# Two batches side by side: attention in phases of its own, and one conversion of a weight chunk per two batches

## The chip, the cores and the metric

The kernel runs on one core of a Trainium2 chip. The metric is the device time of one execution in microseconds (us). The core has a matrix engine (TensorE, PE in the profile), two elementwise engines (VectorE, DVE; ScalarE, ACT), GpSimd (POOL), and SyncE (SP), which here only issues transfers (DMA).

## The reference

Four batches of 448 tokens go through sigmoid attention with 12 heads of 64, a token-shift block with gate, and a mixer over tokens and channels.

```python
scores = scale * np.matmul(q, k.transpose(0, 1, 3, 2)) - np.log(S)
attn = 1.0 / (1.0 + np.exp(-scores))
x = heads side by side of np.matmul(attn, v)              # (4, 448, 768)
xk = mu_k * x + (1.0 - mu_k) * x_prev                     # x_prev: x one token earlier
xr = mu_r * x + (1.0 - mu_r) * x_prev
k = np.maximum(xk @ w_k, 0.0)                             # (448, 1024)
x = 1.0 / (1.0 + np.exp(-(xr @ w_r))) * (k * k @ w_v)     # (448, 768)
h = np.maximum(x.transpose(0, 2, 1) @ w_tok1, 0.0) @ w_tok2
u = x + h.transpose(0, 2, 1)
out = u + np.maximum(u @ w_ch1, 0.0) @ w_ch2              # 768 -> 1536 -> 768
```

`w_k` and `w_r`, `w_v`, `w_tok1`, `w_tok2`, `w_ch1`, `w_ch2` come as 64-bit numbers and are turned into 32-bit ones on the chip.

## The kernel before, in words

Activations lie with channels on the 128 partitions and tokens along the columns; 448 columns are one batch. A product of two 32-bit matrices is made of three matmuls: each operand is split into a high part (rounded for the matmul's number type) and a low part (the rest), and high x high, high x low and low x high are summed in PSUM (lines 339, 341 and 342, `products`). Activations as operands are the tiles `Ah`/`Al` and `Mh`/`Ml`, weights `whi`/`wlo`.

Weights come in 52 chunks of 128 output columns (38 of them 128 x 768, 14 of 128 x 512). A chunk passes five steps: load of the 64-bit words (`raw`), two ACT operations that take them apart (`narrow_1`, lines 189 and 190), two DVE operations that join them (`narrow_2`, 193 and 196), ACT's copy to the high part (251), DVE's subtraction to the low part (256). Before, the first use of a chunk passes all five and stores the joined 32-bit chunk in DRAM (`kept`); later uses load it from there and pass the last two. `weights()` hands out the next chunk and lets the steps of the chunks behind it advance.

Stages ahead of the channels run per batch (`first_part`): r (w_r, 6 chunks), k (w_k, 8 chunks; relu, square, split), w_v (12 chunks of 512 rows, two per row of output, with transposes of the finished rows in between, line 392; in the last three batches two of six rows are transposed by DVE and small DMAs instead, `y_turn`), first token product (tok1), second token product (tok2). Channel mixing (`second_part`, ch1 and ch2 in two halves) runs for two batches side by side, in pieces of 512 and 384 columns; the first batch's rows wait in DRAM (`away`).

Attention: a unit is one pair of heads of one batch, 24 in all. `unit_qk` makes scores for 128 keys of both heads into a `psc` buffer (2 buffers) and ACT makes the sigmoid (line 154); `unit_av` multiplies by the values (163). Batch 0's attention runs first, by itself; the units of the later batches are put between the products by a planner (`spread`, `run`) that counts the time of the matmuls issued. Each engine runs its instructions in the order written; SP issues all transfers in order.

Of the kernel before, what the change touches and what calls it, by code (L numbers as in the profile page):

```python
# [47 lines left out]
BLK = 32
# [3 lines left out]
def kernel(  # L52
# [16 lines left out]

# [9 lines left out]
    const, big = pool("const", 1), pool("big", 1)  # L79
    wraw, wpool, wsplit = pool("wraw", 4), pool("wpool", 4), pool("wsplit", 3)  # L80
    dram = pool("dram", 1, space=bass.MemoryType.DRAM)
    tmps, tmp2 = pool("tmps", 4), pool("tmp2", 2)
    a3, a7 = pool("a3", 3), pool("a7", 7)
# [3 lines left out]
    def ENG(kind, b):  # L87
        return DVE if (kind, b) in ONDVE else ACT

    def split(hi, lo, src, engine):  # L90
        if engine is ACT:
            ACT.copy(hi, src)  # L92
        else:
            DVE.tensor_copy(hi, src)  # L94
        DVE.tensor_tensor(out=lo, in0=src, in1=hi.bitcast(F32), op=ALU.subtract)  # L95
# [4 lines left out]
    kns, qns, vns = {}, {}, {}  # L100

    def load_kq(g):
        if g < B * NPAIR:
            kns[g] = a3.tile([P, 4 * P], F32, tag="kn", name="kn")
            SP.dma_start(out=kns[g], in_=k[g])
            qns[g] = a3.tile([P, S], F32, tag="qn", name="qn")
            SP.dma_start(out=qns[g], in_=q[g])

    def load_v(g):
        if g < B * NPAIR:  # L110
            vns[g] = a3.tile([P, 2, 4, D], F32, tag="vn", name="vn")
# [15 lines left out]
    load_kq(1)  # L127

# [4 lines left out]
    for name, src in (("k", mu_k), ("r", mu_r)):  # L133
# [4 lines left out]
        mus[name] = (m, om)  # L138


    xe = big.tile([P, NT, 1 + S], F32, tag="xe", name="xe")
    POOL.memset(xe[:, :, 0:1], 0.0)

    att = {}

    def unit_qk(b, pr, chunks):
        g = b * NPAIR + pr
        for c in chunks:
            ps = ps_sc.tile([P, 2, 512], F32, tag="sc", name="psc")
            for h in range(2):  # L150
                me = slice(h * D, h * D + D)
                PE.matmul(ps[:, h, :S], kns[g][me, c * P : (c + 1) * P], qns[g][me], start=True, stop=True)  # L152
            a = a7.tile([P, 2, S], F32, tag="a", name="a")
            ACT.activation(a, ps[:, :, :S], AF.Sigmoid, bias=-math.log(S), scale=1.0 / math.sqrt(D))  # L154
            att[(g, c)] = a

    def unit_av(b, pr):
        g = b * NPAIR + pr
        ps = ps_av.tile([P, 512], F32, tag="av", name="pav")
        for c in range(4):  # L160
            a = att.pop((g, c))
            for h in range(2):
                PE.matmul(ps[h * D : h * D + D, :S], vns[g][:, h, c], a[:, h], start=(c == 0), stop=(c == 3))  # L163
        ACT.copy(xe[:, pr, 1:], ps[:, :S])

    def burst(b, pr):
        g = b * NPAIR + pr
        unit_qk(b, pr, (0, 1))
        load_kq(g + 2)
        load_v(g + 1)  # L170
        if pr:
            unit_av(b, pr - 1)
# [521 lines left out]
```

## Time and profile before

| | |
|---|---|
| median of 3 runs | 956.77 us (956.35 to 959.75) |
| the profiled execution | 958.75 us, its span 957.0 us |
| busy in the span | PE 918.9, weight loads 731.8 (they overlap PE), DVE 481.3, ACT 400.2 us |
| moved by DMA | 133.22 MB |

A matmul's busy time includes its way through the array and overlaps the next one's, so the time that one costs in a sequence is read from the distance of two starts. PEclk is the granted clock of TensorE as a share of 2.4 GHz.

### The profile page before, as it was taken

How to read it: one execution, taken by the hardware profiler on the slowest of the kernel's cores; microseconds unless marked ns; L12 is line 12 of the kernel's file. 1: busy time of each engine (PE TensorE's matmuls, PEld its weight loads, DVE VectorE, ACT ScalarE, POOL GpSimd, SP SyncE). 2: the span in 40 equal slices, each digit the busy share in tenths (PEclk: the TensorE clock that was granted, in tenths of full speed). 3: DMA queues.
4: the chain of work that ended last, by engine and by line, in shares of the span. 5: the costliest groups of instructions: out<-in, count | busy, mean ns of one | idle time of the engine just before them, and what ended most of it. 6: DMA issues, size and time to landing. Idle time of an engine off the chain costs nothing.

```text
span 957.0 us, 11625 instructions
## 1 busy us (share of the span) xinstructions
PE 918.9 (96%) x4484; PEld 731.8 (76%) x4484; DVE 481.3 (50%) x785; ACT 400.2 (42%) x622; POOL 1.3 (0%) x10
## 2 busy tenths in 40 slices
PE   9999998899999899999999999999899899999998
PEld 3367666687796687797988676677799788998987
DVE  3955675783234844444589224435835462232232
ACT  6767666424635654343521444433243342111210
POOL 0000000000000000000000000000000000000000
PEclk9999999999999999999999999999999999999999
DMA  8846556433336643655415532232423422142223
GB/s 290 277 167 230 186 183 208 151 107 114 99 100 214 228 164 131 213 168 197 158 62 179 184 98 87 77 86 67 149 89 87 134 96 68 61 144 69 66 75 106
DMA packets 59767, 133.22 MB, mean 139 GB/s; under 512 B 12352, under 2 KB 26176, under 8 KB 59712
## 3 DMA queue, kind: packets, MB, share of 16 engines
q1 hardware_dynamic: 59712, 132.48, 42.0%
q8 instruction: 35, 0.57, 0.3%
q14 instruction: 20, 0.16, 0.1%
HBM read 101.46 MB, written 29.62 MB: 137 GB/s over the span
## 4 chain that ended last, share of the span: by engine, by line
PE 80%; DVE 13%; ACT 4%; issue 3%; DMA 0%; SPq 0%; DVEq 0%; POOL 0%; ACTq 0%; POOLq 0%
PE psmm L342 21%; PE psmm L339 21%; PE psmm L341 20%; PE pav L163 8%; PE psc L152 8%; DVE wlo L256 3%; DVE mix L329 2%; DVE Al L95 2%; ACT Ah L92 1%; ACT a L154 1%; DVE Ah L94 1%; DVE wd L193 1%; DVE mix L328 1%; DVE r L495 1%; PE psmm L392 1%
## 5 line engine op out<-in xcount | busy, mean ns | idle before, releaser
L342 PE MATMUL psmm<-Ah,wlo 128*128 128x448 f32 (+2 forms) x688 | 250.9, 365 | 15.2 <-DVE wlo L256 15.2
L339 PE MATMUL psmm<-Ah,whi 128*128 128x448 f32 (+2 forms) x688 | 251.9, 366 | 1.9 <-DVE Ah L95 1.0
L341 PE MATMUL psmm<-Al,whi 128*128 128x448 f32 (+2 forms) x672 | 244.2, 363 | 0.2 <-DVE Al L95 0.2
L342 PE MATMUL psmm<-Mh,wlo 128*128 128x448 f32 (+2 forms) x480 | 176.7, 368 | 10.6 <-DVE wlo L256 10.5
L251 ACT CAST whi<-wd 128x768 fp32r<-128x768 f32 (+1 forms) x160 | 120.3, 756 | 138.0 <-PE psmm L341 102.8
L339 PE MATMUL psmm<-Mh,whi 128*128 128x448 f32 (+2 forms) x480 | 177.0, 369 | 0.5 <-DVE r L541 0.5
L341 PE MATMUL psmm<-Ml,whi 128*128 128x448 f32 (+2 forms) x480 | 175.3, 365 | 0.0
L256 DVE TENSOR_TENSOR wlo<-wd,whi 128x768 fp32r<-128x768 f32 (+1 forms) x160 | 136.8, 858 | 49.2 <-ACT whi L251 48.8
L342 PEld LDWEIGHTS psmm<-Ah,wlo 128*128 128x128 f32 x688 | 129.6, 188 | 30.6 <-DVE wlo L256 19.5
L339 PEld LDWEIGHTS psmm<-Ah,whi 128*128 128x128 f32 x688 | 129.6, 188 | 24.6 <-issue 10.5
L341 PEld LDWEIGHTS psmm<-Al,whi 128*128 128x128 f32 x672 | 126.7, 188 | 11.7 <-DVE Al L95 0.7
L342 PEld LDWEIGHTS psmm<-Mh,wlo 128*128 128x128 f32 x480 | 90.5, 188 | 24.5 <-DVE wlo L256 15.7
L154 ACT ACTIVATE a<-psc 128x896 f32<-128x896 f32 x96 | 82.9, 915 | 56.9 <-PE psc L152 56.9
L339 PEld LDWEIGHTS psmm<-Mh,whi 128*128 128x128 f32 x480 | 90.5, 188 | 13.7 <-issue 4.6
L341 PEld LDWEIGHTS psmm<-Ml,whi 128*128 128x128 f32 x480 | 90.6, 189 | 8.5
L152 PE MATMUL psc<-qn,kn 64*128 64x448 f32 x384 | 85.7, 565 | 2.9 <-ACT a L154 2.9
L527 DVE SCALAR_TENSOR_TENSOR Ml<-psmm,Mh 128x512 fp32r<-128x512 f32 (+1 forms) x48 | 29.9, 624 | 110.7 <-ACT Mh L526 110.7
L163 PE MATMUL pav<-a,vn 128*64 128x448 f32 x384 | 77.5, 545 | 0.0
L526 ACT ACTIVATE Mh<-psmm 128x512 fp32r<-128x512 f32 (+1 forms) x48 | 26.1, 544 | 108.2 <-PE psmm L342 108.2
L152 PEld LDWEIGHTS psc<-qn,kn 64*128 64x128 f32 x384 | 32.3, 185 | 48.6 <-issue 31.6
L163 PEld LDWEIGHTS pav<-a,vn 128*64 128x64 f32 x384 | 25.4, 136 | 48.0 <-issue 45.1
L193 DVE SCALAR_TENSOR_TENSOR wd<-wd,raw 128x768 uint32<-128x768 uint32 (+2 forms) x54 | 47.1, 872 | 3.5 <-ACT raw L190 3.4
(62 smaller groups left out, 599.6 us busy)
## 6 DMA issues: line engine op xcount, KB each, us to landing
wd<-w SPq DMA_DIRECT2D x66, 384.0 KB, 3.1
raw<-in_moe_w_ch_dram SPq DMA_DIRECT2D x24, 768.0 KB, 5.1
w<-wd SPq DMA_DIRECT2D x38, 384.0 KB, 3.1
wd<-w SPq DMA_DIRECT2D x42, 256.0 KB, 2.8
kn<-in_k_dram SPq DMA_DIRECT2D x24, 256.0 KB, 4.0
vn<-in_v_dram SPq DMA_DIRECT2D x24, 256.0 KB, 5.1
raw<-in_moe_w_k_dram SPq DMA_DIRECT2D x8, 768.0 KB, 5.9
raw<-in_moe_w_v_dram SPq DMA_DIRECT2D x12, 512.0 KB, 4.0
```

Source lines behind the costliest of these rows:

```text
L95: DVE.tensor_tensor(out=lo, in0=src, in1=hi.bitcast(F32), op=ALU.subtract)
L152: PE.matmul(ps[:, h, :S], kns[g][me, c * P : (c + 1) * P], qns[g][me], start=True, stop=True)
L154: ACT.activation(a, ps[:, :, :S], AF.Sigmoid, bias=-math.log(S), scale=1.0 / math.sqrt(D))
L163: PE.matmul(ps[h * D : h * D + D, :S], vns[g][:, h, c], a[:, h], start=(c == 0), stop=(c == 3))
L193: DVE.scalar_tensor_tensor(out=dst, in0=dst, scalar=3, in1=raw[..., 0], op0=ALU.logical_shift_left, op1=ALU.bitwise_or)
L251: ACT.copy(halves[i][0][:rows, :kt], loads[i])
L256: DVE.tensor_tensor(out=lo, in0=loads.pop(i), in1=f32(hi), op=ALU.subtract)
L339: PE.matmul(ps[:, :n], wh, xh, start=(i == 0), stop=False)
L341: PE.matmul(ps[:, :n], wh, xl, start=False, stop=False)
L342: PE.matmul(ps[:, :n], wl, xh, start=False, stop=(i == count - 1))
L526: ACT.activation(hi, ps[:, :n], AF.Relu)
L527: DVE.scalar_tensor_tensor(out=lo, in0=ps[:, :n], scalar=0.0, in1=f32(hi), op0=ALU.max, op1=ALU.subtract)
```

## The change

Everything from the token shift on runs for two batches side by side: a row of the activations is 896 columns, a chunk of weights is multiplied with all of them (a matmul of 512 columns and one of 384 on the same weights, one after the other), and tok1 takes 512 columns that hold two rows of both batches. The joined chunks are no longer kept in DRAM: each chunk passes all five steps once per two batches, 104 times in all. `ahead` lets the steps of the chunks behind advance after each group of matmuls. PSUM is four buffers of two banks for all uses. Attention has no planner: the 12 units of two batches run one after the other ahead of their stages (`attention`), all four score chunks of a unit, then its values; the sigmoids use the tile `rows`, which is free then. All transposes are PE's. The token-mixed rows stay in SBUF (`rows`, `two`), so `away` and `part` are gone. The tiles `one`, `two` and `three` hold one stage's operand after another.

```diff
-    ps_mm = pool("ps_mm", 3, space=PSUM)
-    ps_av, ps_sc = pool("ps_av", 1, space=PSUM), pool("ps_sc", 2, space=PSUM)
...
+    psum = pool("psum", 4, space=PSUM)
...
+    units = [(b0 + i % 2, i // 2) for b0 in range(0, B, 2) for i in range(2 * NPAIR)]
...
-    kept = [dram.tile([rows, kt * P], F32, tag="w%d" % i, name="w%d" % i) for i, (_, rows, kt) in enumerate(chunk)]
...
-    seq = (seq_a + seq_a + seq_c) * (B // 2)
...
+    seq = (first + second) * (B // 2)
...
-            loads[i] = wpool.tile([P, NT, P], F32, tag="wd", name="wd")[:rows, :kt]
-            if first[i]:
-                narrow_1(loads[i].bitcast(U32), raws[i])
-            else:
-                SP.dma_start(out=loads[i].rearrange("p t n -> p (t n)"), in_=kept[seq[i]])
+        for i, r, kt in step("form", upto):
+            forms[i] = wpool.tile([P, NT, P], F32, tag="wd", name="wd")[:r, :kt]
+            narrow_1(forms[i].bitcast(U32), raws[i])
...
-                stores.append((seq[i], loads[i]))
-
-    def w_store():
-        while stores:
-            c, d = stores.pop(0)
-            SP.dma_start(out=kept[c], in_=d.rearrange("p t n -> p (t n)"))
...
+    def ahead(i):
+        def low_form():
+            w_low(i + 3)
+            w_form(i + 4)
+
+        def join_raw():
+            w_join(i + 4)
+            w_raw(i + 7)
+
+        return [lambda: w_high(i + 3), low_form, lambda: None, join_raw]
...
+    def products(ps, pieces, parts, at=0, count=None, hooks={}):
+        count = count or len(parts)
+        for i, (wh, wl, xh, xl) in enumerate(parts, at):
+            passes = [(wh, xh), (wh, xl), (wl, xh)] if xl is not None else [(wh, xh), (wl, xh)]
+            for n, (w, x) in enumerate(passes):
+                for a, cols in pieces:
+                    PE.matmul(
+                        ps[:, a : a + cols],
+                        w,
+                        x[:, a : a + cols],
+                        start=(i == 0 and n == 0),
+                        stop=(i == count - 1 and n == len(passes) - 1),
+                    )
...
+    def attention(b0):
+        base = b0 * NPAIR
+        for i in range(base, base + 2 * NPAIR):
+            p, t, xe = i - base, (i - base) // 2, xes[(i - base) // 2 % 2]
+            if i + 2 < base + 2 * NPAIR:
+                load_kq(i + 2)
+                if p:
+                    load_v(i + 2)
+            scores(i)
...
+            ps = values(i, xe)
+            if p == 0 and i + 2 < base + 2 * NPAIR:
+                load_v(i + 2)
+            ACT.copy(xe[:, p % 2, 1:], ps[:, :S])
+            if p % 2:
+                mix("r", t, xr, xe)
+                mix("k", t, xk, xe)
...
+            w = weights()
+            ps = new_ps()
+            products(ps, WIDE, against(w, xr, NT))
+            ACT.activation(rows[:, m], ps[:, :W], AF.Sigmoid)
...
         for m in range(F // P):
-            ps = new_mm()
...
+            w = weights()
+            ps = new_ps()
+            products(ps, WIDE, against(w, xk, NT))
+            hi, lo = kk(m)
+            t = tmps.tile([P, W], F32, tag="tmp", name="sq")
+            ACT.activation(t, ps[:, :W], AF.Relu)
+            DVE.tensor_tensor(out=t, in0=t, in1=t, op=ALU.mult)
+            ACT.copy(hi, t)
+            DVE.tensor_tensor(out=lo, in0=t, in1=f32(hi), op=ALU.subtract)
...
         for m in range(NT):
-            ps = new_mm()
...
+            ps = new_ps()
+            for part in range(2):
+                w = weights()
+                parts = [(w[0][:, t], w[1][:, t], *kk(4 * part + t)) for t in range(4)]
+                hooks = {2: lambda: y_transpose(m - 1)} if m and part == 0 else {}
+                products(ps, WIDE, parts, 4 * part, 8, hooks)
+            DVE.tensor_tensor(out=rows[:, m], in0=rows[:, m], in1=ps[:, :W], op=ALU.mult)
...
+        for piece in range(3):
+            ps = new_ps()
+            ms = slice(2 * piece, 2 * piece + 2)
+            for j in range(2):
+                wh, wl = wt1[j]
+                x = [t[:, :, ms].rearrange("p r m b c -> p r (m b c)") for t in y]
+                parts = [(wh[:, r], wl[:, r], x[0][:, r], x[1][:, r] if r < 3 else None) for r in range(4)]
+                products(ps[:, j * 512 : (j + 1) * 512], ((0, 512),), parts)
+                if piece == 0 and j == 0:
+                    y_transpose(NT - 1)
+            hi, lo = (t[:, :, ms].rearrange("p j m b c -> p j (m b c)") for t in h1)
+            psv = ps.rearrange("p (j n) -> p j n", j=2)
+            ACT.activation(hi, psv, AF.Relu)
+            DVE.scalar_tensor_tensor(out=lo, in0=psv, scalar=0.0, in1=f32(hi), op0=ALU.max, op1=ALU.subtract)
...
+        for m in range(NT):
+            ps = new_ps()
+            for b in range(2):
+                parts = [(h1[0][:, j, m, b], h1[1][:, j, m, b], wt2h[:, j], wt2l[:, j]) for j in range(2)]
+                products(ps[:, b * 512 : b * 512 + S], ((0, S),), parts)
+            hi, lo = (beside(p[:, m]) for p in u)
+            r = beside(rows[:, m])
+            DVE.tensor_tensor(out=r, in0=r, in1=banks(ps), op=ALU.add)
+            ACT.copy(hi, r)
+            DVE.tensor_tensor(out=lo, in0=r, in1=f32(hi), op=ALU.subtract)
...
-                    ps = new_mm()
-                    yield from products(ps, n, NT, beside(w, u, NT, at, n))
...
+                ps = new_ps()
+                products(ps, WIDE, against(w, u, NT))
+                hi, lo = (p[:, f] for p in h2)
+                ACT.activation(hi, ps[:, :W], AF.Relu)
+                DVE.scalar_tensor_tensor(
+                    out=lo, in0=ps[:, :W], scalar=0.0, in1=f32(hi), op0=ALU.max, op1=ALU.subtract
+                )
...
+                ps = new_ps()
+                products(ps, WIDE, against(w, h2, 6))
+                DVE.tensor_tensor(out=rows[:, m], in0=rows[:, m], in1=ps[:, :W], op=ALU.add)
...
-                    SP.dma_start(out=out[b0 + 1, m * P : (m + 1) * P], in_=rows[m])
...
-    for b in range(0, B, 2):
-        nxt = {}
-        todo += spread(attention_units(b + 1, [mix_units("r", nxt, b + 1)]), now, now + END_1 * t_a)
...
-            todo += spread(attention_units(b + 2), now + BEG_2 * t_a, t0 + END_2 * t_c)
-            todo += spread(mix_units("r", box, b + 2), t0 + 0.77 * t_c, t0 + 0.86 * t_c)
-            todo += spread(mix_units("k", box, b + 2), t0 + 0.87 * t_c, t0 + 0.97 * t_c)
...
+                    for b in range(2):
+                        SP.dma_start(
+                            out=out[b0 + b, m * P : (m + 1) * P], in_=rows[:, m, b * S : (b + 1) * S]
+                        )
...
+    for b0 in range(0, B, 2):
+        attention(b0)
+        first_part(b0)
+        second_part(b0)
```

Below, the order of instructions on an engine at three places. First PE, before, in the r stage of the first batch (`psc` scores, `pav` values of the unit before, `psmm` products): an attention unit stands between products, as 18 of the 24 do.

```order
L341 MATMUL psmm<-Al,whi 128x448
L342 MATMUL psmm<-Ah,wlo 128x448
L152 MATMUL psc<-qn,kn 128x448 x4
L163 MATMUL pav<-a,vn 64x448 x8
L152 MATMUL psc<-qn,kn 128x448 x4
L339 MATMUL psmm<-Ah,whi 128x448
```

PE of the changed program: the end of the first attention phase (L160 scores, L176 values; all tiles of PSUM are `ps`) and the first products.

```order
L160 MATMUL ps<-qkv 128x448 x8
L176 MATMUL ps<-rows,qkv 64x448 x8
L299 MATMUL ps<-one,whi 128x512
L299 MATMUL ps<-one,whi 128x384
L299 MATMUL ps<-one,whi 128x512
L299 MATMUL ps<-one,whi 128x384
L299 MATMUL ps<-one,wlo 128x512
L299 MATMUL ps<-one,wlo 128x384
```

The scores of a unit now stand whole ahead of its values, no product stands between units, and each weight operand is taken by two matmuls.

Second, DVE in the k stage, before, batch 0 (L94 and L95 split a k row, L256 a chunk's low part, L193 and L196 the join):

```order
L94 CAST Mh_801<-k2_951 128x448
L95 TENSOR_TENSOR Ml_802<-k2_951,Mh_801 128x448
L256 TENSOR_TENSOR wlo_928<-wd_853,whi_927 128x768
L193 SCALAR_TENSOR_TENSOR wd_933<-wd_933,raw_856 128x768
L196 SCALAR_TENSOR_TENSOR wd_933<-raw_856,wd_933 128x768
```

And of the changed program (L371 square, L373 its low part, L244 a chunk's low part, L199 and L202 the join):

```order
L371 TENSOR_TENSOR sq_917<-sq_917 128x896
L373 TENSOR_TENSOR one_75<-sq_917,one_75 128x896
L244 TENSOR_TENSOR wlo_930<-wd_886,whi_929 128x768
L199 SCALAR_TENSOR_TENSOR wd_939<-wd_939,raw_805 128x768
L202 SCALAR_TENSOR_TENSOR wd_939<-raw_805,wd_939 128x768
```

The same three operations on a chunk now stand beside work on 896 columns instead of 448, and do so at every use of a chunk.

Third, DVE at the end of tok2, before, second batch of a pair (L495 adds a row, L95 the low parts of `back`, the other batch's row, and of the row itself):

```order
L495 TENSOR_TENSOR r0_1773<-r0_1773,psmm_2698 128x448
L95 TENSOR_TENSOR Al_193<-back_2706,Ah_192 128x448
L95 TENSOR_TENSOR Al_193<-r0_1773,Ah_192 128x448
L495 TENSOR_TENSOR r1_1774<-r1_1774,psmm_2712 128x448
L95 TENSOR_TENSOR Al_193<-back_2720,Ah_192 128x448
L95 TENSOR_TENSOR Al_193<-r1_1774,Ah_192 128x448
```

And of the changed program (L405 the low part of tok1's last piece, L415 adds, L417 subtracts; ACT's copy to the high part stands between the two on its own engine):

```order
L405 SCALAR_TENSOR_TENSOR one_75<-ps_1864,one_75 128x2x512
L244 TENSOR_TENSOR wlo_1894<-wd_1794,whi_1893 128x768
L199 SCALAR_TENSOR_TENSOR wd_1900<-wd_1900,raw_1752 128x768
L202 SCALAR_TENSOR_TENSOR wd_1900<-raw_1752,wd_1900 128x768
L415 TENSOR_TENSOR rows_78<-rows_78,ps_1889 128x896
L417 TENSOR_TENSOR two_76<-rows_78,two_76 128x896
```

A row's addition and subtraction now follow each other with nothing between them, and a chunk's low part and join stand ahead of the first row.

## Rows read from the trace of the kernel before

**Rows 1.** The page: busy time in us by engine, share of the span, instructions.

```profile
PE 918.9 (96%) x4484; PEld 731.8 (76%) x4484; DVE 481.3 (50%) x785; ACT 400.2 (42%) x622; POOL 1.3 (0%) x10
```

**Rows 2.** Timeline of PE: start us, us, operation; first and last of three stretches.

```profile
568.54 0.36 PE L341 MATMUL psmm<-Al,whi 128*128 128x448 f32 x1
...
574.62 0.36 PE L341 MATMUL psmm<-Al,whi 128*128 128x448 f32 x1
...
783.64 0.34 PE L339 MATMUL psmm<-Ah,whi 128*128 128x384 f32 x1
...
789.90 0.39 PE L339 MATMUL psmm<-Ah,whi 128*128 128x512 f32 x1
...
798.10 0.33 PE L339 MATMUL psmm<-Ah,whi 128*128 128x384 f32 x1
```

**Rows 3.** Timeline of PE: one attention unit between products.

```profile
561.67 1.77 PE L152 MATMUL psc<-qn,kn 64*128 64x448 f32 x8
563.37 3.23 PE L163 MATMUL pav<-a,vn 128*64 128x448 f32 x16
566.53 1.77 PE L152 MATMUL psc<-qn,kn 64*128 64x448 f32 x8
568.24 0.47 PE L339 MATMUL psmm<-Ah,whi 128*128 128x448 f32 x1
```

**Rows 4.** Timeline of PE: four transposes and the product after them.

```profile
144.17 0.60 PE L392 MATMUL psmm<-ident,r 128*128 128x128 f32 x4
144.52 0.45 PE L339 MATMUL psmm<-Mh,whi 128*128 128x448 f32 x1
```

**Rows 5.** Timeline of PE in the first attention phase; in brackets the wait before.

```profile
5.79 1.77 PE L152 MATMUL psc<-qn,kn 64*128 64x448 f32 x8
...
14.78 1.77 PE L152 MATMUL psc<-qn,kn 64*128 64x448 f32 x8
16.82 1.84 PE L152 MATMUL psc<-qn,kn 64*128 64x448 f32 x8 [0.26 <-ACT a L154]
...
21.75 0.65 PE L152 MATMUL psc<-qn,kn 64*128 64x448 f32 x2
```

**Rows 6.** Waits by kind: us in total, times, longest.

```profile
PE psmm L342 <- DVE wlo L256: 25.7, 23, 2.1
```

**Rows 7.** Busy time by stretch; after POOL's: granted clock, DMA share, GB/s.

```profile
6.00:49.00 43.00, 41.29 (x198) 14.94 (x196) 30.95 (x54) 32.42 (x41) 0.00 (x0) 1.00 0.84 292
100.00:105.00 5.00, 3.96 (x12) 3.59 (x13) 4.93 (x8) 2.59 (x4) 0.00 (x0) 0.66 0.46 152
```

**Rows 8.** Groups by line and shape: count, busy us, mean ns; last, a transfer.

```profile
L256 DVE TENSOR_TENSOR wlo<-wd,whi 128x768 fp32r<-128x768 f32 x104 | 98.7, 951 | 37.4 <-ACT whi L251 37.4
L251 ACT CAST whi<-wd 128x768 fp32r<-128x768 f32 x104 | 86.1, 830 | 108.0 <-PE psmm L341 77.9 <-DVE wd L196 18.6 <-issue 11.5
L154 ACT ACTIVATE a<-psc 128x896 f32<-128x896 f32 x96 | 82.9, 915 | 56.9 <-PE psc L152 56.9
L196 DVE SCALAR_TENSOR_TENSOR wd<-raw,wd 128x768 uint32<-128x768 uint32 x38 | 36.4, 958 | 1.3
L189 ACT ACTIVATE wd<-raw 128x768 f32<-128x768 f32 x38 | 34.8, 915 | 0.0
L94 DVE CAST Ah<-mix 128x448 fp32r<-128x448 f32 x48 | 18.9, 394 | 5.3 <-PE psmm L342 3.7
L329 DVE SCALAR_TENSOR_TENSOR mix<-xe,muk,mix 128x448 f32<-128x448 f32 x24 | 16.4, 684 | 0.9
L328 DVE TENSOR_SCALAR mix<-xe,omk 128x448 f32<-128x448 f32 x24 | 10.7, 447 | 0.0
...
raw<-in_moe_w_ch_dram SPq DMA_DIRECT2D x24, 768.0 KB, 5.1
```

**Rows 9.** Timeline: the last addition and the last store.

```profile
953.38 0.56 DVE L544 TENSOR_TENSOR r<-r,psmm 128x384 f32<-128x384 f32 x1 [2.13 <-PE psmm L342]
953.97 0.33 SPq L546 DMA_DIRECT2D out_dram<-r  x1
```

More of the change, by code (lines that the diff above doesn't have):

```diff
@@ new lines, with two_parts @@
+    three = const.tile([P, 4 * W], F32R, tag="three", name="three")
+    rows = const.tile([P, NT, W], F32, tag="rows", name="rows")
+    xes = [const.tile([P, 2, 1 + S], F32, tag="xe%d" % i, name="xe") for i in range(2)]
+    def two_parts(t, kt):
+        n = kt * W
+        return [t[:, i * n : (i + 1) * n].rearrange("p (t n) -> p t n", t=kt) for i in range(2)]
+    xr = h2 = two_parts(one, NT)
+    xk = u = two_parts(two, NT)
+    kk_end = two_parts(three, 2)
+    y = [
+        two[:, i * 8 * C : (i + 1) * 8 * C].rearrange("p (r m b c) -> p r m b c", r=4, m=NT, b=2)
+        for i in range(2)
+    ]
@@ L127 @@
     load_kq(1)
+    load_v(1)
     ident = const.tile([P, P], F32, tag="ident", name="ident")
@@ L138, with scores @@
         mus[name] = (m, om)
-    xe = big.tile([P, NT, 1 + S], F32, tag="xe", name="xe")
-    POOL.memset(xe[:, :, 0:1], 0.0)
+    for t in xes:
+        POOL.memset(t[:, :, 0:1], 0.0)
+    turn = [0]
     att = {}
[L146 to L149, printed above, removed]
+    def scores(i):
+        for c in range(4):
+            ps = new_ps()
             for h in range(2):
                 me = slice(h * D, h * D + D)
[L152 to L155, printed above, removed]
@@ L160, in unit_av, with values @@
+            att[c] = a
+    def values(i, xe):
+        ps = new_ps()
         for c in range(4):
-            a = att.pop((g, c))
             for h in range(2):
[L163 to L172, printed above, removed]
-        unit_qk(b, pr, (2, 3))
@@ L198, in narrow_2 @@
         )
[L200 to L207 removed]
+    first, second = [], []
+    for w in (w_r, w_k, w_v, w_tok1):
+        n, r, cols = w.shape
+        first += [(w[i].bitcast(U32), r, cols // P) for i in range(n)]
     for half in range(2):
[L209 to L212 removed]
+        second += [(w_ch1[half * 6 + f].bitcast(U32), P, NT) for f in range(6)]
+        second += [(w_ch2[2 * m + half].bitcast(U32), P, NT) for m in range(NT)]
+    seq = (first + second) * (B // 2)
     done = dict.fromkeys(("raw", "form", "join", "high", "low"), 0)
[L214 to L215 removed]
+    raws, forms, halves = {}, {}, {}
     def step(name, upto):
@@ new lines, in against, with y_transpose @@
+    def against(w, x, kt):
+        return [(w[0][:, t], w[1][:, t], x[0][:, t], x[1][:, t]) for t in range(kt)]
+    def y_transpose(m):
+        ps = new_ps()
+        psv = ps.rearrange("p (r b c) -> p r b c", r=4, b=2)
+        for r in range(4):
+            n = P if r < 3 else TAIL
+            for b in range(2):
+                PE.transpose(psv[:n, r, b], rows[:, m, b * S + r * P : b * S + r * P + n], ident)
+        hi, lo = (t[:, :, m] for t in y)
+        ACT.copy(hi[:, :3], psv[:, :3])
+        DVE.tensor_tensor(out=lo[:, :3], in0=psv[:, :3], in1=f32(hi[:, :3]), op=ALU.subtract)
+        ACT.copy(hi[:TAIL, 3], psv[:TAIL, 3])
+        DVE.tensor_tensor(out=hi[TAIL:, 3], in0=psv[:TAIL, 3], in1=f32(hi[:TAIL, 3]), op=ALU.subtract)
```

482 lines of the change are left out of this document (131 added, 351 removed).

## The prediction

> **What bounds the kernel now.** I read the page first. TensorE (PE) is busy 918.9 of 957.0 us, DVE as the next 481.3 [rows 1]: to be faster, a change must give PE less to do, or take away what is lost between matmuls. Busy time doesn't tell how much is lost, since matmuls overlap, so I took the pace from the timeline, start to start, in stretches without a wait [rows 2]. A 448-column matmul comes every (574.62 - 568.54)/30 = 0.203 us, a 384-column one every (789.90 - 783.64)/36 = 0.174, a 512-column one every (798.10 - 789.90)/36 = 0.228. Each of them loads its own 128x128 weights, also in those stretches, and the pace follows the columns; so loading isn't the limit.
>
> One head pair's attention in the midst of products takes 568.24 - 561.67 = 6.57 us of PE, scores 1.70 + 1.71 and values 3.16 [rows 3]. Four transposes take 0.35 [rows 4]. With these the whole program without a wait is: start 5.8 (the first score matmul [rows 5]), attention 24 x 6.57 = 157.7, the r, k and w_v stages 1584 x 0.203 = 321.1 (396 matmuls a batch), the token products 176 x 0.174 + 144 x 0.203 = 59.8, channel mixing 864 x (0.228 + 0.174) = 347.1, 72 transposes about 8, tail 4. That is 903.5, so 53 us of the 957.0 are lost. By the list of waits 25.7 of them stand at the matmul that needs a chunk's low part, 23 times [rows 6]: VectorE (DVE) subtracts it too late. Around one of these waits the clock fell: 5 us show a mean of 0.66 of full, 0.34 x 5 = 1.7 us lost [rows 7]. What is left of the 53 are the first attention phase, the refill after each wait, and the changes between products and 18 attention units (568.54 - 568.24 = 0.30 where 0.203 is the pace [rows 2, 3]).
>
> **What the change removes and adds on PE.** The r, k and w_v stages of two batches were 792 matmuls of 448 columns, 160.6 us; now they are 396 pairs of 512 + 384, 396 x 0.402 = 159.1. Channel mixing is 432 pairs as before, 173.5. The first token product becomes 66 x 0.228 = 15.0, the second keeps 72 x 0.203 = 14.6. Sum 362.2 per two batches, 724.4 in all, against 728.0. The new alternation of 512 and 384 on the same weights stands in no row; if a 384-column matmul could not cover the load that follows, a pair would cost at most 2 x 0.228. A run of 36 such matmuls with a load each holds 0.174, so I take 0.402. Transposes: all 96 run on PE again, 12 groups of 8 x 0.088 + 0.1 for the change back = 9.6 us.
>
> **Attention alone.** Its 192 score and 192 value matmuls are the same, 157.7 us if PE never waits. In the first phase of before a unit takes (21.75 - 14.78) = 7.0 us [rows 5], since the two score buffers make the next scores wait for the sigmoid. Now four buffers serve, and all four scores stand ahead of the values. Per unit: the scores end on PE at 3.4 us; ScalarE (ACT) starts at 1.0 and its four sigmoids of 0.915 [rows 8] end near 4.7; PE comes to the values of the fourth chunk at 3.4 + 3 x 0.79 = 5.8. Margin 1.1 us. ACT's remaining work of a unit (a copy of half a sigmoid's size, in some units a conversion of 2 x 0.915) fits before the next unit's first scores are ready at 7.5. DVE mixes once per two units: 2 x (2 x (0.447 + 0.685 + 0.394) + 1.11) = 8.3 of 13.1 us. So 6.57, with 7.0 as the other end: 0 to +10.3 us.
>
> **Weights.** The change doesn't convert less in all: each of 104 uses is now converted in full, where 52 chunks were converted once and 160 split. Per 768-column chunk DVE needs 0.951 + 2 x 0.958 = 2.87 us and ACT 0.830 + 2 x 0.915 = 2.66 [rows 8]; PE holds such a chunk for 18 x 0.402 = 7.23 us, where it held it for 18 x 0.203 = 3.65. That is what should end the waits of rows 6. The tightest stage is the k stage. With proportional prices (896/768, an upper bound): from the chunk's end, relu 0.95 (as the sigmoid of 896 columns), square 2.1 (1.11 on DVE), high copy on ACT 3.1, low part on DVE 4.25, the next chunk's low part 5.2, its join, which waits for ACT's narrowing until 5.9, 7.8. DVE is occupied from 1.0 to 7.8, 6.8 of 7.23 us, and a low part is ready 9 us before PE wants it. So nothing waits, with little to spare. In the w_v stage the transposes of a row wait for DVE's multiplication: by the same count it is ready 2.8 us after the row's last matmul, since a join stands ahead of it, and PE wants it after 9 pairs, 3.6 us. The weights' DMA of 768 KB lands in 5.1 us [rows 8] and is issued three chunks ahead; nothing waits for it.
>
> **A new wait.** After the second token product, DVE adds (1.11), ACT copies 0.97, DVE subtracts (1.11), in order and row by row: 3.29 us a row with hand-overs of 0.05, where PE makes a row in 12 x 0.203 = 2.44. Before, the second operand's subtraction filled the time of ACT's copy. Counted from the end of the first token product: ACT's relu to 1.1, DVE's low part of it to 2.4, then the chunk's low part and join, which wait for ACT's narrowing, to 5.7; the sixth row is ready at 5.7 + 6 x 3.29 = 25.5. PE comes to it at 14.6 + 5 x 1.21 + 0.4 = 21.0. So 4.5 us, twice: 9.0; nothing, if the hand-overs hide in work I count in full: 0 to 9. With waits of up to 1.4 us in a row I also expect one fall of the clock each, 1.7 twice: 3.4 (0 to 3.4).
>
> **The sum.** 5.8 + 157.7 + 724.4 + 9.6 + 9.0 + 3.4 + tail. Tail: 957.0 - 953.38 = 3.6 in before [rows 9]; the last addition is 896 wide (+0.55) and two stores follow (+0.4, an issue of 0.33 and its gap), and 0.2 ahead of it: 4.8. Together 914.7 of span. The profiled execution took 958.75 with its span of 957.0, 1.75 outside; its median lies 2.0 lower. So 914.7 + 1.75 - 2.0 = 914.
>
> **The rivals.**
> A, as above: 914, between 902 (no wait at the new place) and 920. Chance 0.64.
> B, attention alone is paced as in the first phase of before: 914 + 10.3 = 924. For it: the only rows of attention alone show 7.0. Against it: what waited there was a buffer that is now doubled. 0.14.
> C, the waits move: half of the 53 us come back at borders of stages that I count as covered. 914 + 26 = 940. For it: DVE and ACT do more, not less, and hand over to each other more often. 0.10.
> D, slower: DVE falls behind in the products. Place: the matmul that first needs a chunk's low part. It decides when DVE with its waits for ACT needs more than 7.23 us a chunk in the k stage or 9.6 + 0.8 in two w_v chunks; my count is 6.8, so 6% more on each operation reaches it, and then the 9 us of lead are used up. The price at before's mean wait of 25.7/23 = 1.12 us on all 104 chunks is +117: 1031. Above 0.4 us a chunk it is slower than before. 0.06.
> E, the clock falls while attention runs alone, as it no longer has products around it. At half the clock its 157.7 us double: 1072. The rows speak against it: 43 us of attention alone, with PE waiting in each unit, show 1.00 [rows 7]. The Trainium skill (TensorE: Matmul & The Clock Gate, "A second HAM failure mode: psum-queue depth-cycling") says that short idle times between groups of matmuls that cycle through PSUM buffers can make the clock swing between its levels; by that rule the new phases would pay. The trace disagrees for attention and agrees for the waits near 101 us. 0.03.
> The rest, 0.03, is a result within 0.5% or a cause not named.
>
> **How the numbers follow.** The forecast is A's 914. A, B and the better half of C lie in 902 to 940, 0.83 in all. Half a per cent, 4.8 us, is about what a measurement of this kernel can tell from no change. Faster by more: A, B, C, 0.89 with a part of the rest; within it 0.02; slower, D and E, 0.09.
>
> **What the new profile would show.** Right: scores and values alternate at 6.57 us a unit; waits on the chunk's low part are nearly gone; pairs of 512 and 384 come every 0.402; at the start of channel mixing PE waits 3 to 5 us for DVE or ACT; DVE is busy longer than before (104 full conversions). Wrong: a unit of 7 us or more (B), waits for the low part in most chunks of the k and w_v stages (D), a clock below 1 in the attention phases (E), a pair above 0.41 us.

## The result and the profile after

The changed kernel takes **915.09 us** (median of 4 runs, 914.43 to 915.57) against 957.0 us (median of 4, 956.35 to 959.75): a ratio of 0.9556, 95% interval 0.9537 to 0.9576. The forecast was 914, between 902 and 940. The profiled execution took 914.43 us, its span 912.7.

The page, answering to [rows 1], and the row of the granted clock by fortieths of the span:

```profile
PE 900.8 (99%) x4464; PEld 723.8 (79%) x4464; DVE 505.3 (55%) x563; ACT 420.0 (46%) x550; POOL 1.2 (0%) x9
...
PEclk9999999999999999999999999999999999999999
```

DVE and ACT are busy longer than before (505.3 and 420.0 us against 481.3 and 400.2), in a span 44.3 us shorter; PE is now busy in 99% of it. The list below is all of PE's waits (total us, times, longest); the kind that led it before, the chunk's low part [rows 6], isn't in it:

```profile
PE ps L299 <- ACT two L416: 2.3, 4, 0.9
PE ps L299 <- DVE two L417: 1.8, 4, 0.5
PE ps L319 <- DVE rows L382: 1.7, 2, 0.9
PE ps L132 <- POOL rows L129: 1.3, 1, 1.3
```

Busy time by stage (columns as in [rows 7]: the stretch, its length, each engine's busy time, the clock, DMA). The stretches are the first attention phase, r, k, w_v, tok1, and (behind tok2) the first six chunks of channel mixing and the next six:

```profile
5.85:82.43 76.58, 76.58 (x385) 30.46 (x384) 45.68 (x53) 54.71 (x70) 0.00 (x0) 1.00 0.50 165
82.43:126.17 43.74, 43.74 (x218) 39.23 (x217) 24.90 (x29) 19.64 (x27) 0.00 (x0) 1.00 0.33 114
126.17:184.35 58.18, 58.18 (x290) 52.16 (x289) 35.41 (x38) 30.88 (x39) 0.00 (x0) 1.00 0.26 84
184.35:247.13 62.78, 62.78 (x329) 56.47 (x329) 37.12 (x51) 28.58 (x48) 0.00 (x0) 1.00 0.33 103
247.13:264.46 17.33, 16.47 (x75) 13.12 (x75) 9.48 (x10) 5.98 (x8) 0.00 (x0) 1.00 0.35 128
279.18:325.97 46.79, 44.73 (x217) 38.89 (x216) 28.50 (x30) 21.46 (x26) 0.00 (x0) 1.00 0.28 87
325.97:369.60 43.63, 43.63 (x217) 39.15 (x217) 23.24 (x24) 15.68 (x20) 0.00 (x0) 1.00 0.37 121
```

r has 108 pairs of 512 and 384 columns: 43.74/108 = 0.405 us a pair; the six undisturbed chunks of channel mixing 43.63/108 = 0.404 (forecast 0.402). The first six chunks are longer by 46.79 - 43.63 = 3.16 us: that is the new wait. PE doesn't idle in the r, k and w_v stages at all. In tok1 it waits for the last row's multiplication, which ends at 249.57 + 1.08 = 250.65:

```profile
249.57 1.08 DVE L382 TENSOR_TENSOR rows<-rows,ps 128x896 f32<-128x896 f32 x1
```

An attention unit in PE's timeline, answering to [rows 3] and [rows 5]:

```profile
25.15 3.28 PE L160 MATMUL ps<-qkv 64*128 64x448 f32 x16
28.35 3.23 PE L176 MATMUL ps<-rows,qkv 128*64 128x448 f32 x16
31.51 3.28 PE L160 MATMUL ps<-qkv 64*128 64x448 f32 x16
```

A unit is 31.51 - 25.15 = 6.36 us, with no wait in brackets; 12 are 76.6 in the first phase and 533.34 - 456.96 = 76.4 in the second, from this timeline's starts.

A period of the k stage on DVE and ACT (a chunk is 148.25 to 155.52, PE's 7.27 us):

```profile
148.25 0.92 ACT L370 ACTIVATE sq<-ps 128x896 f32<-128x896 f32 x1 [1.96 <-PE ps L299]
149.20 1.09 DVE L371 TENSOR_TENSOR sq<-sq 128x896 f32<-128x896 f32 x1 [0.93 <-ACT sq L370]
150.32 0.94 ACT L372 CAST one<-sq 128x896 fp32r<-128x896 f32 x1 [1.16 <-DVE sq L371]
...
151.29 1.09 DVE L373 TENSOR_TENSOR one<-sq,one 128x896 fp32r<-128x896 f32 x1 [1.01 <-ACT one L372]
...
152.30 0.95 DVE L244 TENSOR_TENSOR wlo<-wd,whi 128x768 fp32r<-128x768 f32 x1
...
153.64 0.96 DVE L199 SCALAR_TENSOR_TENSOR wd<-wd,raw 128x768 uint32<-128x768 uint32 x1 [0.39 <-ACT raw L196]
154.63 0.96 DVE L202 SCALAR_TENSOR_TENSOR wd<-raw,wd 128x768 uint32<-128x768 uint32 x1
```

DVE is occupied, its waits for ACT counted, from 149.20 to 155.59: 6.4 of 7.27 us (forecast 6.8 of 7.23).

The new wait, on PE and behind it on DVE and ACT, and then the tail, answering to [rows 9]:

```profile
282.37 1.08 DVE L415 TENSOR_TENSOR rows<-rows,ps 128x896 f32<-128x896 f32 x1
283.48 0.94 ACT L416 CAST two<-rows 128x896 fp32r<-128x896 f32 x1 [2.16 <-DVE rows L415]
284.45 1.09 DVE L417 TENSOR_TENSOR two<-rows,two 128x896 fp32r<-128x896 f32 x1 [1.01 <-ACT two L416]
...
285.46 1.08 DVE L415 TENSOR_TENSOR rows<-rows,ps 128x896 f32<-128x896 f32 x1
285.60 0.68 PE L299 MATMUL ps<-two,whi 128*128 128x512 f32 x2 [0.46 <-DVE two L417]
...
287.57 0.68 PE L299 MATMUL ps<-two,whi 128*128 128x512 f32 x2 [0.87 <-ACT two L416]
...
907.91 1.09 DVE L434 TENSOR_TENSOR rows<-rows,ps 128x896 f32<-128x896 f32 x1 [6.18 <-PE ps L299]
```

A row of that chain takes 285.46 - 282.37 = 3.09 us on DVE, of which it waits 1.0 for ACT's copy. The tail from the last addition's start to the span's end is 912.7 - 907.9 = 4.8.

**Where the 44.3 us came from.** Over PE's whole timeline, each distance of two starts was taken less the pace of [rows 2], and the excess sorted by what the later matmul waited for. Before: 29.4 us at the low parts (23 times; more than the listed 25.7, since the refill after a wait counts too), 6.2 at other waits, 11.5 in small gaps of refills and changes, 4.1 on the way into attention units; attention itself took 161.6. After: nothing at low parts, 7.9 at the first three waits of the list above; attention 153.0. So 29.4 of the 44.3 is the low parts and 8.6 is attention. The other gaps (refills, changes, ways into attention) are 15.6 before and 7.6 after; less the 1.7 by which the other waits grew, that is the remaining 6. The sums are good to about half a us. What is left cancels: the products' pace takes 4.0 less, the transposes 3.2 more, the tail 1.2 more.

What took the low-part waits away need not be one thing. The change doubles the chunk, but it also moves the attention units, with their mixing and splitting on DVE, out of the products. Before, 12 of the 23 low-part waits, 16.6 of the 25.7 us, have mixing operations (lines 328 and 329) on DVE within the 5 us ahead of them, as here, between 97.86 and the low part:

```profile
97.86 0.45 DVE L328 TENSOR_SCALAR mix<-xe,omr 128x448 f32<-128x448 f32 x1
...
100.03 0.95 DVE L256 TENSOR_TENSOR wlo<-wd,whi 128x768 fp32r<-128x768 f32 x1
...
101.04 0.59 PE L342 MATMUL psmm<-Ah,wlo 128*128 128x448 f32 x1 [1.96 <-DVE wlo L256]
```

The other 11, 9.1 us, have none. No run here has the doubled chunk without the moved attention, or the reverse, so how the 29.4 us divide between the two isn't shown.

### The profile page after: what moved, and what is told of

Its sections match the earlier page's. It is cut to its first block, busy times and chain, and to the rows that moved or that the text cites. A ratio compares the mean times of both kernels' runs of the same rounds, so it can differ in the third digit from the quotient of the medians.

```text
span 912.7 us, 10954 instructions
## 1 busy us (share of the span) xinstructions
PE 900.8 (99%) x4464; PEld 723.8 (79%) x4464; DVE 505.3 (55%) x563; ACT 420.0 (46%) x550; POOL 1.2 (0%) x9
## 4 chain that ended last, share of the span: by engine, by line
PE 92%; DVE 5%; ACT 2%; issue 0%; POOL 0%; ACTq 0%; POOLq 0%
PE ps L299 74%; PE ps L160 8%; PE ps L176 8%; DVE two L417 1%; DVE rows L415 1%; ACT two L416 1%; PE ps L319 1%; DVE wd L199 1%; DVE wd L202 1%; PE ps L132 1%; ACT wd L195 0%; ACT raw L196 0%; DVE rows L382 0%; DVE two L322 0%; ACT whi L240 0%
## 5 line engine op out<-in xcount | busy, mean ns | idle before, releaser
L299 PE MATMUL ps<-one,whi 128*128 128x512 f32 (+1 forms) x1152 | 280.7, 365 | 0.0
L299 PE MATMUL ps<-two,whi 128*128 128x512 f32 (+1 forms) x1044 | 261.8, 367 | 4.1 <-ACT two L416 2.3
L299 PEld LDWEIGHTS ps<-one,whi 128*128 128x128 f32 x1152 | 208.1, 188 | 25.0 <-PE ps L176 0.7
L299 PEld LDWEIGHTS ps<-two,whi 128*128 128x128 f32 x1044 | 189.0, 188 | 30.3 <-ACT two L416 3.8
L299 PE MATMUL ps<-one,wlo 128*128 128x512 f32 x576 | 163.1, 364 | 0.0
L299 PE MATMUL ps<-two,wlo 128*128 128x512 f32 (+1 forms) x528 | 154.8, 367 | 0.0
L244 DVE TENSOR_TENSOR wlo<-wd,whi 128x768 fp32r<-128x768 f32 (+1 forms) x104 | 91.6, 881 | 41.6 <-ACT whi L240 41.6
L299 PEld LDWEIGHTS ps<-one,wlo 128*128 128x128 f32 x576 | 104.4, 188 | 12.0
L199 DVE SCALAR_TENSOR_TENSOR wd<-wd,raw 128x768 uint32<-128x768 uint32 (+1 forms) x104 | 92.3, 887 | 30.5 <-ACT raw L196 27.9
L299 PEld LDWEIGHTS ps<-two,wlo 128*128 128x128 f32 x528 | 96.0, 188 | 12.2
L202 DVE SCALAR_TENSOR_TENSOR wd<-raw,wd 128x768 uint32<-128x768 uint32 (+1 forms) x104 | 92.2, 887 | 3.6
L196 ACT ACTIVATE raw<-raw 128x768 uint32<-128x768 uint32 (+1 forms) x104 | 86.6, 833 | 0.0
L160 PE MATMUL ps<-qkv 64*128 64x448 f32 x384 | 78.9, 550 | 0.0
L176 PE MATMUL ps<-rows,qkv 128*64 128x448 f32 x384 | 77.4, 545 | 0.0
L160 PEld LDWEIGHTS ps<-qkv 64*128 64x128 f32 x384 | 35.3, 188 | 42.8 <-issue 38.0
L176 PEld LDWEIGHTS ps<-rows,qkv 128*64 128x64 f32 x384 | 25.4, 136 | 49.1 <-issue 32.5
```

What stands on the lines that cost most here:

```text
L160: PE.matmul(ps[:, h * 512 : h * 512 + S], kns[i % 3][me, c * P : (c + 1) * P], qns[i % 3][me], start=True, stop=True,)
L176: PE.matmul(ps[h * D : h * D + D, :S], vns[i % 3][:, h, c], att[c][:, h], start=(c == 0), stop=(c == 3))
L196: ACT.activation(raw[..., 0], raw[..., 0], AF.Copy, bias=0.4375, scale=0.875 * 2.0**-29)
L199: DVE.scalar_tensor_tensor(out=dst, in0=dst, scalar=3, in1=raw[..., 0], op0=ALU.logical_shift_left, op1=ALU.bitwise_or)
L202: DVE.scalar_tensor_tensor(out=dst, in0=raw[..., 1], scalar=0x80000000, in1=dst, op0=ALU.bitwise_and, op1=ALU.bitwise_or)
L244: DVE.tensor_tensor(out=halves[i][1], in0=forms.pop(i), in1=f32(halves[i][0]), op=ALU.subtract)
```

## The experiments

Lines of a changed kernel are its own, so numbers can lie a few lines off those above. Each was timed against the kernel before on the same chip; for comparison, the changed kernel's ratio is 0.9556.

**1. The order behind the second token product** (`low_rest` makes the oldest subtraction still to be made).

```diff
...
             DVE.tensor_tensor(out=r, in0=r, in1=banks(ps), op=ALU.add)
             ACT.copy(hi, r)
-            DVE.tensor_tensor(out=lo, in0=r, in1=f32(hi), op=ALU.subtract)
+            rest.append((lo, r, hi))
+            if m:
+                low_rest()
+        low_rest()
```

> The changed kernel with one order changed: after the second token product VectorE adds row m+1 before it subtracts for the low part of row m, so that ScalarE's copy lies between. Theory: the wait at the start of channel mixing is a chain of add, copy and subtraction at 3.10 us a row against PE's 2.45; with the new order VectorE needs 2 x 1.09 = 2.2 us a row and PE sets the pace; the 46.8 us of the first six chunks fall to the 43.6 of the next six, 3.2 us twice: 915 - 6 = 909. Rival: VectorE is simply behind there and the wait moves to the next operand or chunk: 915.

907.42 us, ratio 0.9477 (0.9463 to 0.9491). The trace shows no wait at the start of channel mixing; its first six chunks now run from 278.69 to 322.34, 43.65 us where they took 46.79. So the 3.1 us are the chain through ACT, not DVE's load. Twice 3.14 are 6.3 of the 7.7 us. The other 1.4 may be in part the clock: the mean granted clock of the executions is 0.998 to 0.999 for the changed kernel and 0.999 to 1.000 here, and 0.001 of 913 us is 0.9 us. That is an estimate from rounded numbers, not shown by a trace.

**2. The last row's transposes later.**

```diff
-                if piece == 0 and j == 0:
+                if piece == 0 and j == 1:
                     y_transpose(NT - 1)
```

> The changed kernel with the last row's transposes one group of matmuls later (after the second half of the first piece of the first token product; they are needed for its third piece). Theory: PE reaches them 0.86 and 0.80 us before VectorE's multiplication; 2.4 us later it is long done, so both waits and their refill go: 915 - 2 = 913. Rival: the split of the transposes is then late for the third piece and the wait moves there: 915 or more.

914.58 us (912.0 to 914.99), ratio 0.9541 (0.9524 to 0.9558): by time, not to be told from no change. In the profiled execution (914.99 us) the wait at the transposes is gone from the list, but the clock fell behind the unchanged waits at the start of channel mixing, in both pairs of batches. First this kernel's stretches around the first of the two places, then the same place (a stretch that holds the same four waits) in the changed kernel:

```profile
283.00:287.00 4.00, 2.39 (x8) 1.25 (x8) 2.74 (x3) 1.84 (x4) 0.00 (x0) 1.00 0.00 0
287.00:291.00 4.00, 3.55 (x11) 3.00 (x11) 3.56 (x5) 2.90 (x5) 0.00 (x0) 0.59 0.00 0
291.00:295.00 4.00, 4.00 (x21) 3.62 (x20) 3.33 (x4) 2.14 (x3) 0.00 (x0) 0.98 0.57 197
```

```profile
283.00:287.00 4.00, 2.96 (x12) 1.70 (x11) 2.54 (x3) 1.36 (x2) 0.00 (x0) 1.00 0.00 0
287.00:291.00 4.00, 2.98 (x13) 2.39 (x14) 3.04 (x4) 3.77 (x5) 0.00 (x0) 1.00 0.00 0
291.00:295.00 4.00, 4.00 (x21) 3.58 (x21) 3.38 (x4) 2.42 (x3) 0.00 (x0) 1.00 0.56 161
```

The same waits of 0.3 to 0.9 us are followed by a clock of 0.59 in one execution and of 1.00 in the other. By these rows a fall costs 0.41 x 4 + 0.02 x 4 = 1.7 us. At an equal mean clock of 0.999, this kernel's fastest execution took 912.0 us and the changed kernel's 914.43, so the gain of about 2 us is there where the clock doesn't fall; that rests on one execution of each.

**3. Both, and the last addition in two halves.**

```diff
...
+                        if last:
+                            me = slice(b * S, (b + 1) * S)
+                            DVE.tensor_tensor(out=rows[:, m, me], in0=rows[:, m, me], in1=ps[:, me], op=ALU.add)
...
```

> Both edits together, and the last addition of the program in two halves of 448 columns, the first half's store issued before the second half is added. Theory: the gains are in different places and add up, 6.3 + 2 + 0.4: 906. Rival: a part of them is given back, 909 to 913.

905.18 us, ratio 0.9452 (0.9439 to 0.9466), the fastest kernel here. Its span is 902.8 at a clock of 1.000, and one wait of PE is left in the list, the one at the program's start. All its executions have a mean clock of 1.000: without the waits there was no fall of the clock either. Against experiment 1 it is 2.2 us faster, about the 2.4 expected of the later transposes and the halved last addition.

**4. The lead shortened to that of before.**

```diff
-            w_low(i + 3)
+            w_low(i + 2)
```

> The changed kernel with the low part of a chunk made one chunk later, in the same distance as in the kernel before (while its predecessor is multiplied). Theory: it is the length of a chunk (7.2 us for 768 x 896 where it was 3.65) that covers the bursts on VectorE; in the worst stage the low part ends about 5 us after the chunk's end is passed on VectorE and PE wants it 0.8 us into the next but one, so waits stay away: 914 to 918. Rival: the lead is what ended the waits, not the length; then PE waits for the low part again, 104 chunks by about 0.3 to 1.1 us: 945 or more.

916.55 us, ratio 0.9572 (0.9558 to 0.9585), which overlaps the changed kernel's. In the middle of the k stage a low part is now done 2.8 us ahead of its first matmul, where the changed kernel has 10.1 (forecast 9). One low-part wait came back in 104 chunks:

```profile
PE ps L299 <- DVE wlo L244: 0.5, 1, 0.5
```

**5. A longer lead in the kernel before.**

```diff
-        w_low(i + 2)
         w_high(i + 3)
+        w_low(i + 3)
```

> The kernel before with the low part of a chunk made one chunk earlier, right behind its high part. Theory: the 29 us around its low-part waits come from bursts on VectorE against a lead of one short chunk (3.65 us); a chunk more of lead holds most of them: 957 - 20 = 937, between 930 and 945. Rival: VectorE and ScalarE with one batch per chunk can't keep up in those stages whatever the lead, and only the doubled chunk ends the waits: 952 to 957, or slower, since VectorE then waits for ScalarE's high part.

937.91 us, ratio 0.9795 (0.977 to 0.982). No wait for a low part is left, but others grew (the top of the list):

```profile
PE psmm L392 <- DVE r L451: 5.4, 4, 2.1
...
PE psmm L339 <- DVE r L495: 2.4, 6, 1.1
PE psmm L339 <- ACT whi L251: 2.2, 2, 1.2
```

By the same sum as above, 29.4 us at low parts became nothing, and 6.2 at other waits became 17.2: what DVE did earlier for the weights it did later for the rows.

**6. Conversion at every use, with one batch per chunk** (the kernel before, nothing kept in DRAM).

```diff
-    first = [c not in seq[:i] for i, c in enumerate(seq)]
+    first = [True] * len(seq)
...
-                stores.append((seq[i], loads[i]))
```

> The kernel before with every use of a chunk converted in full from the 64-bit words, nothing kept in DRAM: conversion as in the changed kernel, but for one batch at a time in the stages ahead of the channels. Theory: it is the two batches per chunk that make conversion at every use free. With one, VectorE needs 2.87 + about 1.1 us and ScalarE 2.66 + about 1.5 us for a 768-column chunk of the k stage that PE holds for 3.65, and attention's sigmoids come on top: 30 to 90 us more, 990 to 1050. Rival: conversion hides anyway, since VectorE is busy for half of the span: 950 to 965.

994.84 us, ratio 1.0392 (1.0375 to 1.041). The list of waits is led by

```profile
PE psmm L341 <- DVE wlo L255: 40.6, 29, 3.1
PE psmm L338 <- DVE r L494: 6.4, 10, 1.6
```

although DVE is busy for 66% and ACT for 56% of the span. What the changed kernel does for nothing costs 38 us here. By an estimate 10 of them are the clock (a mean of 0.989 over 992 us, where the kernel before has 0.999 to 1.000 in most executions). The attention units stand between the products in this kernel too, so it doesn't tell the doubled chunk from the moved attention either: 15 of its 29 low-part waits, 25.8 of the 40.6 us, stand within 5 us behind mixing operations.

**7. Half of the conversions taken away from the changed kernel** (the first two batches store the joined chunks in DRAM, the next two load them).

```diff
...
+            if i >= n_all:
+                SP.dma_start(out=forms[i].rearrange("p t n -> p (t n)"), in_=kept[i - n_all])
+            else:
+                narrow_1(forms[i].bitcast(U32), raws[i])
...
```

> The changed kernel with the joined chunks kept in DRAM by the first two batches and loaded from there by the next two, which need no narrowing and joining: VectorE has some 92 us less to do, ScalarE 87, the DMA writes and reads about 19 MB more and reads 37 less. Theory: no wait of PE in products comes from conversion, so taking half of it away gives nothing but the second pair's wait at the last transposes: 914. Rival one: conversion at every use costs time that the waits don't show: 905 or less. Rival two: the round trips through DRAM were part of the cost of the kernel before: 920 or more.

912.42 us, ratio 0.9534 (0.9515 to 0.9553): 91 us less of DVE and 77 less of ACT go with 2.7 us by the medians (2.1 by the ratios), and the intervals overlap. The trace has one of the two waits at the transposes and some of those of channel mixing less (3.4 us in the list for 5.8), as expected of the second pair.

**8 and 9. The low part computed three and five times over** (the same result; `range(5)` in the second).

```diff
-            DVE.tensor_tensor(out=halves[i][1], in0=forms.pop(i), in1=f32(halves[i][0]), op=ALU.subtract)
+            form = forms.pop(i)
+            for _ in range(3):
+                DVE.tensor_tensor(out=halves[i][1], in0=form, in1=f32(halves[i][0]), op=ALU.subtract)
```

> The changed kernel with every chunk's low part computed three times over (same result): two more VectorE operations of 0.95 us (0.69 for the short chunks) a chunk, 183 us of VectorE work in all. Theory: VectorE is off the path. In the k stage it stands idle 0.9 us of 7.27 per chunk, so it falls behind by about 1.0 us a chunk there, 8 us in 8 chunks, which the 9 us of lead just hold; elsewhere it has 2 us or more to spare: 915 to 925. Rival: VectorE is so close to being the bound that what is added goes on the path, at least half of it: 1000 or more.

> The changed kernel with every chunk's low part computed five times over: 367 us of VectorE work more, 871 us in all, still below the span. Theory: what counts is each stage's own balance. VectorE then needs about 10.2 us per 7.27 us chunk in the k stage (2.9 over, 8 chunks, less 9 us of lead: 14), 3 us per row of w_v over (about 10 with waits) and 2 to 3 per six chunks of channel mixing (10), so some 35 to 40 us per two batches: 985, between 960 and 1030. Rival: the average decides, and below the span VectorE hides: 925 to 935.

Three times: 923.75 us, ratio 0.9642 (0.9615 to 0.9669). 175 us more of DVE work (680.0 for 505.3) cost 8.7; no low part is waited for. Of the 8.7 the profiled execution, at 919.70 and a mean clock of 0.997, shows 5.3, with 2.8 us of longer waits in the list; the other three, at clocks of 0.992 to 0.994, took about 4 us more. In the k stage DVE now needs 149.77 - 141.95 = 7.82 us a chunk by the starts of its squares, 0.55 more than PE, and the lead holds that for 8 chunks: the last one's low part is still done 6.0 us ahead of its first matmul (10.1 in the changed kernel). Five times: 1023.51 us, ratio 1.0686 (1.0666 to 1.0707), with DVE at 860.1 us still below the span; a chunk of the k stage takes DVE 149.14 - 139.33 = 9.81 us. The largest of PE's waits:

```profile
PE ps L321 <- DVE rows L384: 31.2, 12, 5.0
PE ps L301 <- DVE wlo L246: 25.0, 15, 2.8
PE ps L301 <- DVE one L429: 11.5, 4, 4.6
```

In the w_v stage DVE paces: its multiplications of two rows start 243.97 - 230.63 = 13.3 us apart, where PE needs 62.78/6 = 10.5:

```profile
230.63 1.08 DVE L384 TENSOR_TENSOR rows<-rows,ps 128x896 f32<-128x896 f32 x1
...
243.97 1.08 DVE L384 TENSOR_TENSOR rows<-rows,ps 128x896 f32<-128x896 f32 x1
```

The granted clock of that stretch (185 to 250 us) is 0.92. The balance of single stages decides, not the share of the span. My estimate of 985 was low by 38: I had not counted the transposes' wait for the rows, the largest kind, nor the clock (a mean of 0.964 of 1024.7 us, some 37).

**10. Two score buffers in attention** (four PSUM buffers, two for scores and two for values; products take them in turn).

```diff
...
     def scores(i):
         for c in range(4):
-            ps = new_ps()
+            ps = new_ps(0)
...
     def values(i, xe):
-        ps = new_ps()
+        ps = new_ps(1)
```

> The changed kernel with the four PSUM buffers dealt two to the scores and two to the values during attention; products go on taking all four in turn. Theory: four buffers are what took attention alone from 7.0 to 6.37 us a unit; with two the third and fourth scores wait for a sigmoid (0.92 us each against 0.8 of scores), a unit takes 6.8 to 7.0 and the whole 24 x 0.5 = 12 us more: 927. Rival: the order (all four scores, then all values) did it, and two buffers do as well: 915.

930.64 us, ratio 0.9729 (0.9699 to 0.9759). A unit has the wait of [rows 5] again:

```profile
43.48 1.83 PE L164 MATMUL ps<-qkv 64*128 64x448 f32 x8 [0.33 <-ACT rows L173]
45.24 3.23 PE L180 MATMUL ps<-rows,qkv 128*64 128x448 f32 x16
48.40 1.77 PE L164 MATMUL ps<-qkv 64*128 64x448 f32 x8
50.49 1.02 PE L164 MATMUL ps<-qkv 64*128 64x448 f32 x4 [0.33 <-ACT rows L173]
```

50.49 - 43.48 = 7.01 us, 0.65 more than with four buffers; 24 x 0.65 = 15.6, and 15.5 were measured by the medians, 16.6 by the ratios.

**11. Scores in two halves around the values of the unit before**, as the kernel before has them, with four buffers (`finish` makes a unit's values and mixing).

```diff
-            scores(i)
+            scores(i, (0, 1))
+            if p:
+                finish(i - 1)
...
+            scores(i, (2, 3))
```

> The changed kernel with attention's groups in the order of the kernel before: two score chunks of a unit, the values of the unit before, the other two score chunks; four buffers as in the changed kernel. Theory: a unit was 6.57 us in the midst of products and is 6.37 now because each change between scores and values costs some 0.1 us and all four scores together need two fewer changes a unit; this order brings 6.57 back, 24 x 0.2 = 4.8, and about 1 us at the end of each phase, where the last values follow their scores at once: 921. Rival: the 0.2 belongs to the changes between attention and products; the unit stays at 6.37: 915 to 917.

916.06 us, ratio 0.9547 (0.9527 to 0.9567): no change. The theory was badly put: when units follow each other, the second half of one and the first half of the next stand together, so PE still makes sixteen score matmuls in a row (as the profile counts them, two records for one instruction):

```profile
39.63 3.28 PE L160 MATMUL ps<-qkv 64*128 64x448 f32 x16
42.83 3.23 PE L176 MATMUL ps<-rows,qkv 128*64 128x448 f32 x16
...
77.82 1.78 PE L160 MATMUL ps<-qkv 64*128 64x448 f32 x8
79.52 3.23 PE L176 MATMUL ps<-rows,qkv 128*64 128x448 f32 x16
```

The one lone group of eight, at the phase's end, takes 79.52 - 77.82 = 1.70 us, as in [rows 3]; sixteen take 3.20. So the 6.57 of before goes with groups of eight that stand between other work.

## Why the prediction was right, step by step

The place of the gain was read rightly. That the total is within 0.2% is partly luck: attention, the new wait and the clock were put 10.8 us too high, the products, the transposes and the wait at them 8.1 too low, and the step from the profiled execution to the median was off by 2.7 the other way.

- **Low parts (rival D's question).** Right that they no longer wait; in part argued as to why. The lead alone (experiment 5) gives 18.5 us in the kernel before; with the lead of before, the doubled chunk and the moved attention together (experiment 4) keep all but some 1.5. Conversion at every use costs 38 us in the arrangement of before and nothing measurable in the new one (experiments 6 and 7). The prediction gave the whole credit to the doubled chunk (7.23 us for 3.65) and didn't count that the mixing leaves the products, though mixing stands ahead of 16.6 of the 25.7 us. D's condition, more than 7.23 us a chunk in the k stage, was met at 7.82 and no low part was waited for, since 8 chunks don't use up the lead; at 9.81 the waits are there (experiments 8 and 9). D's price, a wait on all 104 chunks, wasn't reached even there: 15 times, 25.0 us, behind a larger kind at the transposes.
- **Attention alone: 157.7.** Measured 153.0. The mechanism (four buffers, no wait) is right, and rival B's wait is what two buffers bring: 930.6. The term was 4.7 too high because the 6.57 of a unit between products was taken for that of a unit among its like: it holds two lone groups of eight, at 0.1 us more each.
- **Products.** A pair is 0.404 to 0.405 instead of 0.402: 1656 pairs, some 4 us more. A group of eight transposes in w_v, with what the products beside it lose, is (62.78 - 144 x 0.404)/5 = 0.92 us instead of 0.8: 1.4 more in 12 groups.
- **The transposes' wait for DVE's multiplication.** I counted a margin of 0.8 us in w_v, and there it held. At the last row it did not: in w_v 9 pairs of the next row, 3.6 us, stand ahead of the transposes, but ahead of the last row's stand 11 matmuls of tok1, 2.5 us, less than my own 2.8 for DVE. I had the numbers and didn't apply them to that row. The 2.8 is too low there as well: the join ahead of the multiplication is that of a 768-column chunk of ch1, and the multiplication ends at 250.65, 3.5 us behind the start of tok1 at 247.13. The cost is 1.7 us listed, 17.33 - 66 x 0.228 - 0.92 = 1.4 us each time with the refill.
- **The new wait: 9.0.** Measured 2 x 3.16 = 6.3. Place and chain are right (experiment 1); a row takes 3.09, not 3.29, since DVE's operations are a little shorter and follow each other closer than I took them to; six rows by 0.2 us are 1.2 of the 1.3 us that each wait was put too high.
- **The clock: 3.4.** None in the profiled execution. A fall did come at this very place in the execution profiled for experiment 2, so the term is an expected value at most, not a fixed cost.
- **Start, tail, outside.** 5.85, 4.8 and 1.73 as said; the median lies 0.7 above the profiled execution here, not 2.0 below.

Rival C, that waits move instead of going, did not happen to the changed kernel but is what happened to the kernel before in experiment 5, where 11 of 29 us came back. Rival E is excluded: the changed kernel's first attention phase shows a clock of 1.00 (first row of the stages). Even in experiment 10, where PE waits in every unit, the stretch shows

```profile
8.00:88.00 80.00, 76.21 (x366) 26.80 (x366) 45.67 (x53) 55.09 (x70) 0.00 (x0) 1.00 0.46 150
```

a clock of 1.00. The Trainium skill (TensorE: Matmul & The Clock Gate, "A second HAM failure mode: psum-queue depth-cycling") has the clock swing where PE idles shortly between groups that cycle through PSUM buffers. This row disagrees with it for waits of 0.33 us once per 7 us. The windows of experiment 2 show such a swing behind four waits of 0.3 to 0.9 us close together, in one execution and not in the other; those are waits for operands, not for buffers.

## What to carry to other kernels

When the matrix engine waits for operands that another engine prepares, first compare that engine's chain per operand, its waits counted, with the time that the operand keeps the matrix engine busy, stage by stage; more columns per operand give all preparing engines more time at once, and so does moving other work of theirs out of the stage (here both came together); a longer lead only holds bursts and may pass the wait on to whatever is queued behind. A chain add, copy, subtract over two engines is paced by the hand-over; putting the next row's first step ahead of this row's last one costs one list and gave 0.8%. Check every border of stages with the same numbers as the stages' middles: all the waits left after this change stood at borders.

## What was not expected of the hardware

The clock after equal waits differs between executions: 0.59 and 1.00 in the same stretch of four microseconds at the same four waits (experiment 2); a change that takes away 2 us can so measure as nothing. And a lone group of eight score matmuls takes 1.70 us where sixteen in a row take 3.20; what the 0.1 us is stays open.
